# Attention weights loaded by transposing DMA: halves of 2048 columns (rows of 4 KB) in place of quarters of 1024

## The chip, the cores and the metric

The kernel runs on one core of one Trainium2 chip. The metric is the device time of one execution in microseconds (us). The kernel before takes 1625.06 us, the median of 3 runs (1622.38 to 1628.38). In what follows, SBUF is the core's working memory, PSUM the eight accumulator banks that TensorE writes, and the granted clock the share of the full TensorE clock that the profile records. A load lands when its last byte has arrived.

## The reference, cut to what matters

Two layers of a segment-recurrent attention (part A) alternate with two gated feed-forward blocks (part B). Part A walks over 64 segments of 32 tokens and hands 8 memory rows from one segment to the next, which makes a long serial chain.

```python
def _A_ref(x, mem0, Wq, Wk, Wv, Wo, seg_len):      # Wq, Wk, Wv: (448, 16, 256); Wo: (16, 256, 448); bf16
    mem = mem0
    for s in range(n_seg):                         # 64 segments
        h = jnp.concatenate([mem, x[:, s * 32:(s + 1) * 32]], axis=1)
        q, k, v = (jnp.einsum('btd,dhe->bhte', h, W) for W in (Wq, Wk, Wv))
        p = softmax(masked(q @ k) / 16)
        o = jnp.einsum('bhte,hed->btd', p @ v, Wo)
        mem = o[:, :8]                             # to the next segment
        ...
x = x + A(layernorm(x)); x = x + B(layernorm(x)); x = x + A(layernorm(x)); x = x + B(layernorm(x))
```

## The kernel before

The kernel never forms q, k and v. In a set-up it folds the weights, head by head, into M = Wq Wk^T and N = Wv Wo, and then works with M and N only. Both products contract over a head's 256 columns, so Wq, Wk and Wv are needed with those columns on the partitions. A transposing DMA does that on the way in. Each of the three matrices arrives in four pieces of 1024 columns (four heads), Wo in four plain pieces, all issued by SyncE on one queue.

```python
        def load_t(w, q):
            S.q.add("dma", ("sp",), {"sp": 3600.0}, lambda E: E.dma_start_transpose(out=st[w, q], in_=src[w][:, q * 1024:(q + 1) * 1024]),
                    (), [(w, q)], name=f"{w}{q}", lat=2500.0)

        def load_o(q, wr=()):
            S.q.add("dma", ("sp",), {"sp": 3000.0}, lambda E: E.dma_start(st["Wo", q], S.Wo_d[:, q * 8:q * 8 + 8, :]),
                    (), [("Wo", q)] + list(wr), name=f"Wo{q}", lat=2500.0)
        # ... cut ...
        for q in range(4):
            load_t("Wq", q)
            load_t("Wk", q)
        # ... cut: small loads, masks, and the products of M, for pairs of heads i = 0..7, each of which
        #     reads ("Wq", i // 2) and ("Wk", i // 2) ...
        for q in range(4):
            load_t("Wv", q)
            load_o(q, [("Wk", q)] if q > 1 else [])     # Wo 2 and 3 take the place of Wk 2 and 3
        def n_main(q):
            for h in range(4 * q, 4 * q + 4):
                for kt in range(3):
                    T = S.tile("R", 1)                  # one of the eight PSUM banks
                    S.mm(lambda T=T, h=h, kt=kt: full("Wv", "Wo", h, kt, T), 2 * S.pitch(D), [("Wv", q), ("Wo", q)], T.res() + [("stage",)])
                    S.cp(...)                           # ScalarE or VectorE moves the bank into N
```

Nothing runs in the order in which it is written. Every operation is put into a list with what it reads and writes and with a guess of its cost in ns (`3600.0` above is the guess for a quarter). A list scheduler on the host then plays these costs through and fixes the order of each engine's instructions:

```python
    def program(self):
        self.q = _Order(self.sc)
        self.setup()
        for t in range(NSTEP):
            self.step(t)
        self.q.run()        # the order of every engine, from the cost guesses
        self.q.emit()       # instructions and semaphore waits, in that order
```

So a changed cost guess may reorder every engine, even where no instruction changed. Three small transposes follow the same queue in every step, from SBUF to SBUF: `xAT` and `xBT` (normalised tokens) and `PTs` (softmax rows).

## Time and profile before

| | before |
|---|---|
| median of 3 runs | 1625.06 us |
| span of the profiled run | 1622.9 us |
| TensorE busy | 95% |
| SyncE issues without a gap | 0.74 to 59.6 us |
| first product of M | 11.19 us |
| first product of N | 42.94 us |
| first product that uses N (N x UTm, where UTm holds rows of h weighted by the softmax) | 78.77 us |

The last three rows are the landmarks; everything up to the last of them is called the set-up.

From the page of before: the span, the busy time of TensorE ("PE": us, share, instructions), and then rows of 40 equal slices of 40.6 us each, busy tenths for TensorE and GB/s of the DMA engines.

```profile
span 1622.9 us, 67486 instructions
...
PE 1548.5 (95%) x30194; PEld 1116.4 (69%) x30194; DVE 1071.2 (66%) x2987; ACT 717.3 (44%) x2164; POOL 90.6 (6%) x156
...
PE   6889999999999999999999999999999999999996
...
GB/s 220 209 79 22 14 16 16 19 18 14 15 19 15 17 16 19 18 14 18 15 15 17 16 19 18 15 14 18 15 17 18 16 19 14 18 14 14 17 21 16
```

TensorE is busy for 90% or more from the third slice to the last but one; only the first two slices leave room, and there alone the DMA row shows more than 200 GB/s. The loads of Wq, Wk, Wv and Wo are all in them.

From the timeline of SyncE of before. Columns: start us, how long SyncE was held by the issue, queue, line, operation, tiles, count.

```profile
0.74 3.96 SPq L534 DMA_TRANSPOSE Nw<-in_A_Wq_dram  x1
4.76 4.29 SPq L534 DMA_TRANSPOSE Nw<-in_A_Wk_dram  x1
...
32.66 4.58 SPq L534 DMA_TRANSPOSE big<-in_A_Wv_dram  x1
37.28 0.59 SPq L538 DMA_DIRECT2D big<-in_A_Wo_dram  x1
37.92 6.20 SPq L534 DMA_TRANSPOSE big<-in_A_Wv_dram  x1
44.17 0.58 SPq L538 DMA_DIRECT2D Nw<-in_A_Wo_dram  x1
...
59.08 0.53 SPq L538 DMA_DIRECT2D big<-in_A_Wo_dram  x1
59.65 2.20 SPq L764 DMA_TRANSPOSE xAT<-xn  x1
```

SyncE is held for about 4 us by each quarter; the first, with no load ahead of it, is held as long as the others, and the profile does not show what holds it. From 32.66 us on quarters alternate with plain Wo loads (0.6 us of issue), and each quarter that has a Wo load ahead of it holds SyncE for 6 to 7 us.

From the timeline of TensorE of before. Columns: start, duration, engine, line, operation, out<-in, shape, count, and in brackets how long TensorE had been idle and what ended it.

```profile
11.19 5.89 PE L128 MATMUL b<-Nw 128*128 128x448 bf16 x18 [4.62 <-DMA Nw<-in_A_Wk_dram]
...
29.78 5.82 PE L128 MATMUL b<-big,Nw 128*128 128x448 bf16 x32
36.49 5.80 PE L128 MATMUL b<-big,Nw 128*128 128x448 bf16 x32 [0.90 <-issue]
42.94 4.70 PE L128 MATMUL b<-big 128*128 128x448 bf16 x24 [0.64 <-issue]
50.66 6.78 PE L128 MATMUL b<-Nw,big 128*128 128x448 bf16 x28 [3.02 <-issue]
...
66.35 0.24 PE L128 MATMUL b<-hT,Mw 128*128 128x40 bf16 x3 [0.26 <-DVE hT L703]
...
78.77 1.51 PE L128 MATMUL b<-Nw,UTm 128*32 128x448 bf16 x28 [0.64 <-ACT UTm L702]
```

The products of M begin when the first Wk quarter has landed (11.19). Those of the fourth quarter wait 0.90 us (36.49), those of N 0.64 us for Wo 0 and 3.02 us for Wo 1. "issue" there means that the profile shows no releaser; the moment fits the landing of the load named. At 66.35 the first step begins.

### The profile page before, as it was taken

How to read it: one execution, taken by the hardware profiler on the slowest of the kernel's cores; microseconds unless marked ns; L12 is line 12 of the kernel's file. 1: busy time of each engine (PE TensorE's matmuls, PEld its weight loads, DVE VectorE, ACT ScalarE, POOL GpSimd, SP SyncE). 2: the span in 40 equal slices, each digit the busy share in tenths (PEclk: the TensorE clock that was granted, in tenths of full speed). 3: DMA queues.
4: the chain of work that ended last, by engine and by line, in shares of the span. 5: the costliest groups of instructions: out<-in, count | busy, mean ns of one | idle time of the engine just before them, and what ended most of it. 6: DMA issues, size and time to landing. Idle time of an engine off the chain costs nothing. (4 is left out here: it accounts for less than half of the span.)

```text
span 1622.9 us, 67486 instructions
## 1 busy us (share of the span) xinstructions
PE 1548.5 (95%) x30194; PEld 1116.4 (69%) x30194; DVE 1071.2 (66%) x2987; ACT 717.3 (44%) x2164; POOL 90.6 (6%) x156
## 2 busy tenths in 40 slices
PE   6889999999999999999999999999999999999996
PEld 2456767767766777677667776776677777766675
DVE  8646767666666676666675766666667666666554
ACT  5524434444443454445443444444444444534332
POOL 3100000000000000000000000000000000000000
PEclk9989999999999999999999999999999999999998
DMA  9821000100000000000000000000000000000010
GB/s 220 209 79 22 14 16 16 19 18 14 15 19 15 17 16 19 18 14 18 15 15 17 16 19 18 15 14 18 15 17 18 16 19 14 18 14 14 17 21 16
DMA packets 130289, 45.46 MB, mean 28 GB/s; under 512 B 119113, under 2 KB 129105, under 8 KB 130001
## 3 DMA queue, kind: packets, MB, share of 16 engines
q1 hardware_dynamic: 129648, 40.92, 11.8%
q8 instruction: 238, 3.90, 1.0%
q14 instruction: 51, 0.41, 0.1%
q10 hardware_dynamic: 352, 0.24, 0.1%
HBM read 10.33 MB, written 1.84 MB: 7 GB/s over the span
## 5 line engine op out<-in xcount | busy, mean ns | idle before, releaser
L128 PE MATMUL b<-hT,Mw 128*128 128x80 bf16 (+1 forms) x11424 | 440.6, 200 | 10.4 <-DVE big L703 7.8
L128 PEld LDWEIGHTS b<-hT,Mw 128*128 128x128 bf16 x11424 | 418.6, 100 | 33.2 <-DVE big L703 13.1
L128 PE MATMUL b<-Nw,big 128*64 128x448 bf16 (+1 forms) x1936 | 309.3, 357 | 4.5 <-issue 3.0
L128 PE MATMUL b<-xBT,big 128*128 128x128 bf16 (+1 forms) x3920 | 216.1, 216 | 9.6 <-DMA xBT<-xn 9.0
L128 PEld LDWEIGHTS b<-xBT,big 128*128 128x128 bf16 x3920 | 205.9, 99 | 11.7 <-DMA xBT<-xn 10.6
L703 DVE CAST TTs<-b 128x320 bf16<-128x320 f32 (+5 forms) x423 | 192.2, 454 | 31.9 <-PE b L128 30.9
L702 ACT ACTIVATE TTs<-b 64x256 bf16<-64x256 f32 (+4 forms) x461 | 191.7, 416 | 39.7 <-PE b L128 31.5
L128 PEld LDWEIGHTS b<-Nw,big 128*64 128x64 bf16 (+1 forms) x1936 | 127.2, 104 | 115.5 <-issue 24.7
L128 PE MATMUL b<-Nw,UTm 128*32 128x448 bf16 x3752 | 191.6, 355 | 1.4 <-ACT UTm L702 1.3
L702 ACT ACTIVATE TTm<-b 128x80 bf16<-128x80 f32 (+5 forms) x400 | 91.7, 229 | 224.6 <-PE b L128 223.8
L703 DVE CAST TTm<-b 128x80 bf16<-128x80 f32 (+5 forms) x484 | 111.9, 231 | 110.4 <-PE b L128 104.8
L128 PEld LDWEIGHTS b<-Nw,UTm 128*32 128x32 bf16 x3752 | 97.6, 97 | 90.1 <-issue 18.9
L703 POOL COPY hK<-xn 32x448 bf16<-32x448 bf16 x136 | 75.6, 556 | 1423.4 <-DVE xn L739 1417.1
L128 PE MATMUL b<-hT,M 64*128 64x80 bf16 (+3 forms) x3808 | 139.9, 197 | 6.8 <-DVE TTs L703 3.7
L703 DVE CAST big<-b 128x512 bf16<-128x512 f32 (+1 forms) x163 | 107.3, 675 | 58.3 <-PE b L128 57.2
L703 DVE CAST UTm<-b 128x448 bf16<-128x448 f32 (+2 forms) x107 | 64.8, 615 | 101.2 <-PE b L128 99.9
L1086 ACT ACTIVATE gT<-b 128x256 bf16<-128x256 f32 x227 | 85.5, 379 | 104.4 <-PE b L128 79.2
L128 PEld LDWEIGHTS b<-hT,M 64*128 64x128 bf16 (+1 forms) x3808 | 105.8, 97 | 22.3 <-DVE hT L703 6.7
L1087 DVE TENSOR_TENSOR hB<-gT,b 128x256 bf16<-128x256 bf16 x227 | 90.6, 411 | 42.9 <-ACT gT L1086 37.5
L702 ACT ACTIVATE big<-b 128x512 bf16<-128x512 f32 (+1 forms) x225 | 106.4, 514 | 8.4 <-PE b L128 7.5
L946 ACT ACTIVATE hi<-b 128x448 bf16<-128x448 f32 x67 | 36.4, 543 | 145.5 <-PE b L128 143.8
L702 ACT ACTIVATE UTm<-b 128x448 bf16<-128x448 f32 (+2 forms) x144 | 76.3, 552 | 39.3 <-PE b L128 37.5
(100 smaller groups left out, 1522.4 us busy)
## 6 DMA issues: line engine op xcount, KB each, us to landing
big<-in_A_Wo_dram SPq DMA_DIRECT2D x3, 896.0 KB, 5.9
out_dram<-ys SPq DMA_DIRECT2D x32, 56.0 KB, 1.9
big<-in_B_W_down_dram SPq DMA_DIRECT2D x1, 1568.0 KB, 7.1
XA<-in_A_x_dram SPq DMA_DIRECT2D x28, 56.0 KB, 2.2
big<-in_B_W_up_dram SPq DMA_DIRECT2D x1, 1344.0 KB, 7.5
big<-in_B_W_gate_dram SPq DMA_DIRECT2D x1, 1344.0 KB, 8.9
PTs<-Ps SPq DMA_TRANSPOSE x68, 2.4
Nw<-in_A_Wo_dram SPq DMA_DIRECT2D x1, 896.0 KB, 6.4
```

Of the source, the lines that this page charges most:

```text
L128: ins = E.matmul(out, lhsT=lhsT, rhs=rhs, **kw)
L702: return E.activation(out(), src(), ACT.Copy)
L703: return E.tensor_copy(out(), src())
L946: S.act(lambda E: E.activation(S.hi[:, :], C.b()[:, 0:D], ACT.Copy), D, C.res(), [("hi",)])
L1086: S.act(lambda E, k=k, R=R, n=n: E.activation(S.gT[:, k % 2, 0:n], R[0].b()[:, 0:n], ACT.Relu), n, R[0].res(), [("gT", k % 2)])
L1087: S.dve(lambda E, k=k, R=R, n=n, fcs=fcs: E.tensor_tensor(S.hB[:, fcs[0]:fcs[-1] + 1, 0:w], S.gT[:, k % 2, 0:n].rearrange("p (a b) -> p a ...
```

## The change

The intent: rows of 4 KB in place of 2 KB, and half as many transposes. A half covers eight heads. The cost guess of a half is 5300, less than two quarters at 3600.

```diff
-        def load_t(w, q):
-            S.q.add("dma", ("sp",), {"sp": 3600.0}, lambda E: E.dma_start_transpose(out=st[w, q], in_=src[w][:, q * 1024:(q + 1) * 1024]),
-                    (), [(w, q)], name=f"{w}{q}", lat=2500.0)
+        def load_t(w, i):
+
+            both = {"Wq": NW[:, 4 * i * W8:(4 * i + 2) * W8], "Wk": NW[:, 2 * W8:4 * W8] if i == 0 else BG[:, 0:2 * W8],
+                    "Wv": BG[:, (2 * i + 2) * W8:(2 * i + 4) * W8]}[w].rearrange("p (k d) -> p k d", k=16)
+            S.q.add("dma", ("sp",), {"sp": 5300.0}, lambda E: E.dma_start_transpose(out=both, in_=src[w][:, i * 2048:(i + 1) * 2048]),
+                    (), [(w, 2 * i), (w, 2 * i + 1)], name=f"{w}{i}", lat=2500.0)
...
-        for q in range(4):
-            load_t("Wq", q)
-            load_t("Wk", q)
+        for i in range(2):
+            load_t("Wq", i)
+            load_t("Wk", i)
...
         for q in range(4):
-            load_t("Wv", q)
+            if q % 2 == 0:
+                load_t("Wv", q // 2)
             load_o(q, [("Wk", q)] if q > 1 else [])
```

## The prediction

> **What bounds the kernel now.** TensorE is busy 95% of the 1622.9 us span (busy shares). The change touches only the set-up, about the first 78 us, in which Wq, Wk, Wv arrive transposed in twelve quarters and Wo in four plain loads, all issued by SyncE, which the timeline shows issuing without a gap from 0.74 to 59.6 us.
>
> A Wq or Wk quarter (0.92 MB) takes 4.0 us of the queue (eight from 0.74 to 32.6 us) and lands 6 to 7 us after its issue. Fine slices of the DMA row show about 290 GB/s for 3.2 us, then a dip of 0.7 to 0.9 us. Small transposes fit: 32 tiles of 4 KB take 1.2 us, 224 tiles 4.0, so roughly 0.75 us fixed and 14.4 ns a tile.
>
> TensorE's waits on these loads (its timeline): until 11.19 us for the first products; 0.9 us at 36.5 (Wk quarter 3); 0.6 at 42.9 (Wo 0); 3.0 at 50.6 (Wo 1, behind a Wv quarter); 0.7 at 58.2; 0.5 at 65.5 (Wo 3). After 35 us that is 5.8 us. Another 2.9 us, before 20 us, is not a load's: the PSUM banks are full while VectorE builds masks until 18.8.
>
> **What the change does.** Six transposes of 1.84 MB replace twelve. Six fixed parts fall away, about 4.5 us. If the rate per tile stays, a half takes 0.75 + 448 x 14.4 ns = 7.2 us instead of 8.05. The rows double to 4 KB: the Trainium skill, "DMA: Bandwidth & Descriptors", section "Latency and other measured facts", gives 261 GB/s for a transpose that misses the 4 KB concatenation of its reads, 350 to 400 for a contiguous one. At 350 a half would take 5.9 us. The trace of before (229 GB/s, dips included) agrees with the low figure; no run yet shows the high one. My estimate: 6.3 us a half.
>
> Against it: the first product needs both first halves and starts at about 15.5 us, not 11.2.
>
> **On the critical path.** The later start should be nearly free: PSUM is evacuated only from 18.8 us, when the banks will just be full. Then the M stage runs at the pace of TensorE and the evacuation (2.9 us per pair of heads). The second Wk half lands at about 28 us, before it is needed (29.8). Wv and Wo then come ahead of TensorE, and the 5.8 us of waits mostly vanish. No more can be gained there, since TensorE is then the limit. At 7.2 us a half, Wk's second lands at about 32 and the gain falls to 3. What follows (Wd, Wg, first PTs) moves forward with the last N product.
>
> So 5 to 6 us: **1619 us, 80% range 1611 to 1626**. Faster by over 2%: 0.01; within 2%: 0.98; slower by over 2%: 0.01.
>
> **What would show it.** SyncE's timeline: a Wq or Wk half takes 6 to 7 us (right) or over 7.5 (no gain). DMA row: longer plateaus, at 290 GB/s (fixed cost only) or about 350 (rows). First product at 15 to 16 us; M stage ending near 42; no TensorE wait over 1 us from 36 to 66; the last N product 6 us earlier than 77.4; from 120 us on the same work, shifted.
>
> **What would make it wrong.** The instruction order is computed from cost guesses; new costs may reorder the whole program, a few us either way. Masks may still be built late, with M's evacuation pushed back. The granted clock dips to 0.5 in stretches from 84 to 102 us, and other stalls may move those dips. The times of before spread over 6 us.

## The result, and the profile after

| | before | after |
|---|---|---|
| median, same rounds, 6 runs each | 1625.31 us | 1627.15 us |
| range | 1622.29 to 1628.38 | 1622.5 to 1631.49 |
| span of the profiled run | 1622.9 us | 1625.2 us |
| first product of M | 11.19 us | 18.55 us |
| first product of N | 42.94 us | 47.63 us |
| first product that uses N | 78.77 us | 78.61 us |
| first output row issued | 266.76 us | 269.18 us |

The ratio is 1.0014 with a 95% interval of 0.9992 to 1.0036: the same. A ratio is the mean time of one kernel's fast runs over that of the other's of the same rounds, so it is not quite the ratio of the medians. A later repeat of both kernels gave 1.0025 (1.0006 to 1.0043). By these two ratios the change costs 2 to 4 us (only the second interval excludes no difference), where 5 to 6 us less had been forecast.

From the page of after, the same lines:

```profile
span 1625.2 us, 67481 instructions
...
PE 1546.5 (95%) x30194; PEld 1117.4 (69%) x30194; DVE 1070.6 (66%) x2988; ACT 719.7 (44%) x2163; POOL 91.0 (6%) x156
...
PE   4989999999999999999999999999999999999996
...
GB/s 234 197 77 21 13 17 16 19 16 16 15 19 14 18 16 19 18 14 18 15 16 17 16 19 18 14 15 19 15 17 16 19 19 14 17 14 14 17 21 16
```

The first slice has less TensorE work (4 tenths in place of 6), the second more (9 in place of 8). These shares do not say where the time went; the timelines do. The DMA row moved 234 GB/s in the first slice against 220.

From the timeline of SyncE of after:

```profile
0.74 7.82 SPq L537 DMA_TRANSPOSE Nw<-in_A_Wq_dram  x1
8.61 7.53 SPq L537 DMA_TRANSPOSE Nw<-in_A_Wk_dram  x1
...
31.75 6.96 SPq L537 DMA_TRANSPOSE big<-in_A_Wv_dram  x1
...
40.01 11.29 SPq L537 DMA_TRANSPOSE big<-in_A_Wv_dram  x1
...
52.59 10.22 SPq L768 DMA_TRANSPOSE xAT<-xn  x2
```

A half of Wq or Wk holds SyncE for 7.5 to 7.8 us, 7.75 from issue to issue on average (the four take 0.74 to 31.75 us). Two quarters took 8.0 (the eight take 0.74 to 32.66). So the halves are hardly faster per byte.

From the timeline of TensorE of after:

```profile
18.55 13.30 PE L128 MATMUL b<-Nw 128*128 128x448 bf16 x64 [12.03 <-DMA Nw<-in_A_Wk_dram]
34.56 13.14 PE L128 MATMUL b<-big,Nw 128*128 128x448 bf16 x64 [2.71 <-issue]
47.63 4.71 PE L128 MATMUL b<-big 128*128 128x448 bf16 x24
52.18 5.20 PE L128 MATMUL b<-Nw,big 128*128 128x448 bf16 x28
...
60.26 0.42 PE L128 MATMUL b<-hT,M 64*128 64x40 bf16 x20 [0.82 <-DVE hT L707]
...
78.61 1.70 PE L128 MATMUL b<-Nw,UTm 128*32 128x448 bf16 x32 [0.64 <-ACT UTm L706]
```

The first product comes 7.4 us later than before. The second Wk half is missing for 2.71 us at 34.56, and from there on all four remaining head pairs (64 products, 13.14 us) still have to be done, where in before only two pairs (5.80 us) stood behind the last landing. M therefore ends 5.4 us later (47.7 against 42.3); 1.6 us of this are a half-clock stretch, as the same 64 products took 11.55 us in another profile (after_again below). In exchange the waits for Wo are gone: N starts at 47.63 and runs on. At 60.26 there is something that the old profile does not have: TensorE turns to the first step before it has done N's third quarter, and waits for the copy of `xAT`. The first product with N then comes at the same time as before.

### The profile page after: what moved, and what is told of

Read it like the earlier page. It is cut to its first block, busy times and chain, and to the rows that moved or that the text cites. A ratio compares the mean times of both kernels' runs of the same rounds, so it can differ in the third digit from the quotient of the medians.

```text
span 1625.2 us, 67481 instructions
## 1 busy us (share of the span) xinstructions
PE 1546.5 (95%) x30194; PEld 1117.4 (69%) x30194; DVE 1070.6 (66%) x2988; ACT 719.7 (44%) x2163; POOL 91.0 (6%) x156
## 3 DMA queue, kind: packets, MB, share of 16 engines
q1 hardware_dynamic: 129456, 40.92, 11.6%
## 5 line engine op out<-in xcount | busy, mean ns | idle before, releaser
L706 ACT ACTIVATE TTs<-b 64x256 bf16<-64x256 f32 (+4 forms) x461 | 191.6, 416 | 38.8 <-PE b L128 30.7
```

Of the source, the lines that this page charges most:

```text
L706: return E.activation(out(), src(), ACT.Copy)
```

## The experiments

Four explanations stood at the start. **A (grain):** a half costs nearly two quarters, and coarser arrival leaves more work behind the last landing of M, while the stage of Wv and Wo wins about as much. **B (order):** the loads did bring a gain, and the order that came with the new guess of 5300 ate it. **C (rows):** rows of 4 KB stream faster, and the kernel merely hides it. **D (clock):** a wait of TensorE costs twice, because the granted clock drops after it. A fifth, **E**, came out of an experiment.

To separate loads from order, most kernels below keep the scheduler's result of before for all engines and rewrite only the list of SyncE's loads afterwards:

```diff
         self.q.run()
+        self.reshape_loads()     # merges quarters of HALVES into halves, or permutes the loads; nothing else
         self.q.emit()
```

A comparison of the instructions in the traces confirms for each of these that TensorE, VectorE, ScalarE and GpSimd have the same order as before (f_v_fill adds its 18 products), and that SyncE differs in the loads alone.

### f_all_halves: all halves, old order

```diff
+    HALVES = ("Wq", "Wk", "Wv")
```

> All twelve quarters become six halves, but every other engine keeps the instruction order of before exactly. Theory A (arrival grain: a half takes twice a quarter's time less about 0.35 us, so the rows of 4 KB buy nothing; the last Wk half has four head pairs of work behind it where the last quarter had two, which costs 5 us in the M stage; the Wv/Wo stage then wins the same back): halves of Wq/Wk occupy the queue 7.6 to 7.8 us, first weight product at 18.5 us, M stage ends at 47.5, first product of N with UTm at about 78.6 to 79 us (before 78.77), time equal to before within 0.3%. Theory B (the gain was there and was eaten by the new order that the new cost guess 5300 brought): with the old order the first UTm product comes at 73 to 76 us and the time falls by 3 to 5 us.

Measured: median 1625.62 us, ratio 0.9991 (0.9963 to 1.0018). First product 18.54, first of N 45.35, first with N **75.96 us**. Theory A alone had said 78.6 to 79, and missed; theory B's 73 to 76 holds, while the 3 to 5 us less in the time that it also named are not seen (the ratio stands for 1.5 us less, with an interval from 6 less to 3 more). With the old order the halves do bring the set-up forward.

### f_qk_halves and f_v_halves: one part of the change each

```diff
+    HALVES = ("Wq", "Wk")        # f_qk_halves
+    HALVES = ("Wv",)             # f_v_halves
```

> Only Wq and Wk come in halves, Wv stays in quarters; all other engines in the order of before. Theory A: the M stage ends at about 47.5 us as in the changed kernel (before 42.3), the Wv/Wo stage has hardly any wait left because it starts late, so the first UTm product is at 78.5 to 80 us: no gain, at most 1 us loss. Theory B: as f_all_halves, some gain.

> Only Wv comes in halves, with Wo 0 and 1, then 2 and 3, in one go behind them; Wq and Wk stay in quarters; all other engines in the order of before. Theory A: M stage ends at 42.3 us as before, N products start at about 45 us (before 42.9) as Wo 0 now waits for a half, but then run without the 3.0 us wait; last N product about 73.5, first UTm product 75.5 to 76.5 us (before 78.77): 2 to 3 us saved, 0.15% of the time. Theory B predicts the same as for f_all_halves here.

Measured: f_qk_halves has its first N product at 44.15 and the first with N at 76.70 us, 2.1 us before the kernel before: better than expected (ratio 0.9985, 0.995 to 1.0019). f_v_halves has them at 45.96 and 79.03: worse than expected by 3 us (ratio 1.0005, 0.9979 to 1.0031). The reason for that miss stands in the next two views of f_v_halves: one line of TensorE's timeline, and two stretches of 4 us (columns: stretch, length, busy us and count of each engine, granted clock, DMA share, GB/s).

```profile
45.96 7.17 PE L128 MATMUL b<-big 128*128 128x448 bf16 x24 [3.93 <-issue]
```

```profile
44.00:48.00 4.00, 2.04 (x6) 0.89 (x7) 0.34 (x1) 0.54 (x1) 0.00 (x0) 0.52 1.13 345
48.00:52.00 4.00, 4.00 (x14) 1.70 (x13) 1.87 (x4) 1.63 (x3) 0.00 (x0) 0.62 1.24 279
```

TensorE waited 3.93 us for Wo 0, and then the 24 products of N's first quarter took 7.17 us. In before they took 4.70. The granted clock was 0.52 and 0.62 in these stretches.

### f_v_fill: TensorE kept busy through that wait

The same kernel with 18 idle products into the PSUM tile that the first real N product overwrites:

```diff
                 if o.kind == "pe":
+                    if o.cat == "first N":   # 18 products of 448 columns, reading Wq 3 and Wk 3, before the wait for Wo 0
+                        self.sc.pe(self.filler(o), [("Wq", 3), ("Wk", 3)], res(o.wr))
```

> f_v_halves plus 18 idle products (448 columns, 3.4 us in all) that TensorE does before it waits for the first Wo, into the PSUM tile that the first real N product overwrites. In f_v_halves the wait of 3.93 us there was followed by a stretch of 6.8 us at granted clock 0.5, in which 24 N products took 7.17 us in place of 4.7. Theory D (the stall costs twice, once as the wait and once more as the lower clock that follows it): with the fillers the clock stays at 1, the 24 products take 4.7 us and the first UTm product comes at 76 to 77 us (79.03 without). If the lower clock has another cause, 79 us as before.

```profile
45.72 4.70 PE L128 MATMUL b<-big 128*128 128x448 bf16 x24 [0.69 <-DMA big<-in_A_Wo_dram]
```

```profile
44.00:48.00 4.00, 3.31 (x19) 1.52 (x18) 1.19 (x2) 1.27 (x3) 0.00 (x0) 1.00 1.17 307
48.00:52.00 4.00, 4.00 (x23) 2.08 (x22) 3.20 (x7) 2.93 (x6) 0.00 (x0) 1.00 1.27 290
```

The same 24 products took 4.70 us at clock 1.00, and the first product with N came at 77.09 us in place of 79.03. Theory D holds for this wait: of the cost of the stall, 2.5 us were the clock. The Trainium skill, "TensorE: Matmul & The Clock Gate", Part 1, says that the clock falls to half after an idle window of about 3.4 us. The traces agree with the half (0.5 in the clock record) and with such a window (the low stretches here are 3.4 us or multiples of it), but not with idle, as after_again below shows.

But the whole run took **1654.37 us**, ratio 1.0193 (1.0167 to 1.022): slower by 1.9%, with an interval that reaches over 2%. Nothing in the steady part differs from f_v_halves in order. This is taken up below (theory E).

### f_grouped: the order of the loads alone

```diff
+    GROUP = ["Wv0", "Wv1", "Wo0", "Wo1", "Wv2", "Wv3", "Wo2", "Wo3"]     # quarters, all
```

> All loads stay quarters of 1024 columns; only SyncE's issue order changes to Wv0 Wv1 Wo0 Wo1 Wv2 Wv3 Wo2 Wo3, the order that the halves bring by themselves. Theory A1 (the Wv/Wo stage gains because there are fewer turns from a transpose to a plain load and back, each a dip of the DMA row): as f_v_halves less 0.7 us, first UTm product at 76 to 77 us, no row of 4 KB needed. Rival A2 (it gains because a half is itself cheaper there): first UTm product at 78 to 79 us, as before.

Measured: first of N 46.31, with N 79.66 us, ratio 0.999 (0.9966 to 1.0013). Neither number fits. N's start was again delayed, here by a wait of 4.30 us for Wo 0, and again a half-clock stretch followed (24 products in 7.45 us). So grouping is not free: the first Wo comes behind two Wv quarters. What it saves in turns between transposes and plain loads is measured without such disturbance in the next run.

### loads_alone: the disputed cost by itself

A kernel that does nothing but load, group after group, each group landed before the next begins. Its output is wrong, which doesn't matter for the time.

```python
for n in (1024, 2048, 4096, 512, 1024, 2048):  group(Wq and Wk in transposes of n columns)      # 7.3 MB each
for _ in range(2):  group(T P T P T P T P); group(T T P P T T P P); group(H P P H P P)          # 7.3 MB each
group(P P P P)
```

> Nothing but weight loads, in groups that land before the next starts; the output is zeros, wrong on purpose. Groups of 7.3 MB of Wq and Wk in transposes of 1024, 2048, 4096, 512, 1024, 2048 columns; then 7.3 MB of Wv and Wo as T P T P T P T P, T T P P T T P P, H P P H P P (T a quarter, H a half, P a plain Wo load), each twice; then P P P P. Theory A (the rate inside a transpose is fixed at about 290 GB/s whatever the row; wider pieces save only the dip between two transposes): groups of 1024 take 8 x 4.0 = 32 us, of 2048 4 x 7.5 = 30, of 4096 2 x 14.3 = 29, of 512 16 x 2.4 = 38; plateaus 290 GB/s in all. Theory C (rows of 4 KB stream faster, and the whole kernel only hides it): groups of 2048 and 4096 take 22 to 25 us with plateaus near 350. Turns between transposes and plain loads cost dips: T P alternating about 27 us plus the final landing, T T P P about 25, H P P about 24.

Measured, from the first issue of a group to that of the next (one look, state unknown):

| group | us | per half, or two quarters |
|---|---|---|
| 16 transposes of 512 | 37.68 | |
| 8 of 1024 (quarters) | 32.81 and 32.41 | 8.2 and 8.1 |
| 4 of 2048 (halves) | 30.96 and 30.17 | 7.7 and 7.5 |
| 2 of 4096 | 28.52 | |
| T P T P T P T P | 30.21 and 30.86 | |
| T T P P T T P P | 28.75 and 28.83 | |
| H P P H P P | 27.40 and 27.52 | |

One line each of the DMA row over a window of this run: quarters (0 to 20 us, slices of 0.5 us), then 4096 columns (65 to 92 us, slices of 0.68 us), then plain loads and the output (358 to 388 us, slices of 0.75 us).

```profile
GB/s 0 0 0 0 87 230 291 288 274 290 290 155 85 220 289 280 268 292 283 120 192 289 276 209 264 291 237 112 125 290 289 289 289 292 208 109 231 290 263 230
```

```profile
GB/s 0 104 286 273 291 290 291 291 289 291 290 291 291 290 289 291 290 291 290 289 144 78 286 291 291 290 289 290 291 291 289 290 290 291 291 289 291 290 290 291
```

```profile
GB/s 289 290 120 276 326 336 344 382 382 240 47 6 0 81 238 381 381 378 381 378 379 382 381 379 382 381 354 38 0 200 257 213 247 214 245 225 236 228 231 153
```

With quarters the row reaches 290 and falls every 4 us. With 4096 columns it stays at 290. It never goes over 292 in either, and the groups of 512 and of 2048 columns reach the same 290. Plain loads reach 380. So the rate inside a transpose does not depend on the row from 1 to 8 KB, and a wider piece saves only the dip between two transposes. Theory C is refuted. The groups with Wo came out 3 to 4 us longer than expected, in the expected order: fewer turns are worth 1.4 to 2.1 us per 7.3 MB, halves about another 1.4. From one issue to the next within a group, a half took 6.6 to 7.6 us here, 7.1 on average, where the halves of Wq and Wk in the whole kernels took 7.0 to 8.0.

### after_again: the changed kernel once more

> The changed kernel unaltered, for a second profile and a better mean. If the half-clock stretch after the 2.7 us wait for the second Wk half (35.8 us) comes by chance, its first UTm product will now be at 76 to 77 us; if that wait always brings it, at 78.6 us again. In the time: ratio 0.998 to 1.002.

Measured: median 1628.52, ratio 1.0025 (1.0006 to 1.0043). From TensorE's timeline of this profile:

```profile
33.16 11.55 PE L128 MATMUL b<-big,Nw 128*128 128x448 bf16 x64 [1.19 <-issue]
44.65 4.71 PE L128 MATMUL b<-big 128*128 128x448 bf16 x24
...
60.64 0.52 PE L128 MATMUL b<-hT,M 64*128 64x40 bf16 x20 [4.18 <-DVE hT L707]
...
81.16 2.83 PE L128 MATMUL b<-Nw,UTm 128*32 128x448 bf16 x56 [0.64 <-ACT UTm L706]
```

This time the wait for Wk was 1.19 us, no half clock followed it, and M's second part took 11.55 us (13.14 in the first profile). N started at 44.65, 3 us earlier. And still the first product with N came at **81.16**, later than in the first profile and than either expectation. All that was won was lost in one wait of 4.18 us at 60.64, on the copy of `xAT`. The clock was at half for 6.8 us from 60.0 us. In both profiles the first step begins at 60.3 to 60.6 us: that is when `xAT` has landed, behind Wv and Wo on the queue, and TensorE's order does not let it do N's third quarter meanwhile.

Whether half clock follows a wait is less a matter of chance than it looks. In the 17 profiles of whole kernels, all 112 half-clock stretches begin on a grid with steps of 3.413 us that is fixed within a profile (in before at 19.75, 50.47, 84.61 and 91.43 us, which are 9, 10 and 2 steps apart). Between the first product of M and 66 us, half clock followed all 19 steps in which TensorE was busy for 46% of the time or less, and of the steps at 48% or more only those that were at half clock themselves. The wait of 2.71 us in after lay mostly in one step (36% busy); the 2.90 us in after_cost were shared by two (56 and 59%), and no half clock followed. The shares use the modelled ends of products, and the bound holds for the large products of the set-up alone.

### f_order_only: the new order with the old loads

The changed kernel's order for TensorE, VectorE, ScalarE and GpSimd; loads as quarters, issued in the order of before.

```diff
         self.q.run()             # with load_t as in the changed kernel
+        self.split_loads()       # each half back into two quarters, SyncE's order of before
         self.q.emit()
```

> The converse: TensorE, VectorE, ScalarE and GpSimd in the order of the changed kernel, but the loads as quarters and issued in the order of before. Theory B2: TensorE waits for the first transposed x, which lands at about 66 us here, before N's third quarter, so the first UTm product comes at 83 to 86 us and the time is 4 to 7 us above before. If the order is harmless: 78 to 79 us.

```profile
64.15 0.51 PE L128 MATMUL b<-hT,M 64*128 64x40 bf16 x20 [7.38 <-DVE hT L741]
...
83.72 2.83 PE L128 MATMUL b<-Nw,UTm 128*32 128x448 bf16 x56 [0.64 <-ACT UTm L740]
```

Measured: first of N 41.85, then 7.38 us of waiting for `xAT`; first with N at **83.72 us**; median 1630.37, ratio **1.0040** (1.0021 to 1.006). By the ratio the new order alone costs about 6 us (3 to 10). Theory B's mechanism is shown, with its place.

### after_cost: the change with an honest guess

```diff
-            S.q.add("dma", ("sp",), {"sp": 5300.0}, ...
+            S.q.add("dma", ("sp",), {"sp": 7700.0}, ...
```

> The changed kernel with one number altered: the cost guess of a half is 7700 ns, which is what a half takes, instead of 5300, so the instruction order is computed from arrival times that the chip keeps. Theory B2 (half of what the change lost is the order: the guess of 5300 makes TensorE stand before N's third quarter waiting for the first transposed x, which lands only at 60 us): no TensorE wait on that transpose over 1 us, first UTm product at 75.5 to 77 us (78.6 and 81.2 in the two profiles of the changed kernel, 78.77 before), time 2 to 4 us below the changed kernel. If the order does not matter: 78.5 to 81 us and the same time.

Measured: no wait on `xAT`, first with N at 76.89 us (78.61 and 81.16 with the guess of 5300), median 1626.44, ratio 1.0006 (0.9992 to 1.0019). The wait is removed by this one number. By the ratios the time is 1 to 3 us better than that of the changed kernel (1.0014 and 1.0025), which the overlapping intervals do not make certain, and it is not better than before.

### f_mixed: first halves, then quarters

The one candidate that the findings suggested: coarse where TensorE cannot start anyway, fine where M's tail hangs on it, and halves for Wv.

```diff
+    HALVES = (("Wq", 0), ("Wk", 0), ("Wv", 0), ("Wv", 1))
```

> Wq and Wk: the first half as one piece, the second in quarters; Wv in halves; all other engines in the order of before. Theory A (grain: the last arrival decides, with the work behind it): first product at 17.8 to 18.5 us, no wait before the third quarter's heads, M stage ends at 43.5 to 44 us (f_all_halves 45.3), N products without a wait over 0.5 us, first UTm product at 74.3 to 75 us (before 78.77, f_all_halves 75.96). In the time 3 to 4 us less than before, 0.2%, just at what five rounds resolve.

Measured: M ran without a wait and ended at 43.55, as expected; but Wo 0 was missing for 1.86 us and N started at 45.41. First with N 77.08 (expected 74.3 to 75). Median 1627.97, ratio 1.0021 (1.0002 to 1.004). It does not beat before, and its interval overlaps those of the changed kernel.

### f_all_again and f_qk_again: does the earlier set-up reach the end?

> f_all_halves unaltered, for a second profile and a better mean: halves for all weights with the order of before. If its earlier first UTm product (75.96 us, 77.5 to 78.8 with quarters in the order of before) is real and reaches the end: again 75.5 to 77 us, and a ratio of 0.997 to 0.9995. If it is given back on the way to 267 us (a late transposed xB, stretches at half clock): the early product again, but a ratio of 0.9995 to 1.001.

> f_qk_halves unaltered (halves for Wq and Wk alone, order of before), the same question: first UTm product 76 to 77.5 us, ratio 0.9975 to 1.0 if the gain reaches the end. Both hypotheses leave the sum of set-up terms as it is; only what follows differs.

Measured: f_all_again has the first product with N at 76.61 and a ratio of 1.0009 (0.9993 to 1.0025); f_qk_again 76.03 and 1.0005 (0.9987 to 1.0022). So the earlier product is real, and no gain is seen at the end. But 1.8 us are 0.11% of the time, and these intervals reach 0.16% or more to each side: they cannot say for certain that it is lost. By landmarks, each as us from the landmark before:

| profile | first with N | to first output row | to 29th output row | to the end |
|---|---|---|---|---|
| before | 78.77 | 187.99 | 1297.13 | 59.0 |
| after | 78.61 | 190.57 | 1297.42 | 58.6 |
| after_again | 81.16 | 188.98 | 1297.42 | 58.3 |
| f_all_halves | 75.96 | 190.35 | 1297.08 | 58.3 |
| f_all_again | 76.61 | 191.21 | 1297.45 | 60.7 |
| f_qk_halves | 76.70 | 188.00 | 1297.99 | 58.6 |
| f_qk_again | 76.03 | 188.95 | 1298.34 | 59.2 |
| after_cost | 76.89 | 191.47 | 1300.46 | 58.0 |
| f_order_only | 83.72 | 186.10 | 1297.68 | 59.6 |

With all halves, the stretch to the first output row is 2.4 to 3.2 us longer than in before. This may be scatter: in the four shift runs below, which keep quarters and the order of before, it is 186.6 to 191.3 us. One place of a loss is seen in the traces. From the views of tile `xBT` between 115 and 135 us (time from issue to landing, the first of its kind), of before, and then of f_all_again with TensorE's line:

```profile
DMA to landing us min/median/max: 2.4/2.4/2.4
```

```profile
DMA to landing us min/median/max: 3.9/3.9/3.9
```

```profile
128.20 3.34 PE L128 MATMUL b<-xBT,big 128*128 128x64 bf16 x64 [1.32 <-DMA xBT<-xn]
```

In before this small transpose landed in 2.4 us and TensorE did not wait. In f_all_again, in f_all_halves and in after it took 3.9 us, TensorE waited 1.26 to 1.32 us, and a half-clock stretch of 3.4 us followed (the granted clock from 120 to 132 us was 0.86 in all three, 1.00 in before). In these three a fetch of 16 KB of instructions began 1.8 to 1.9 us after the issue of `xBT`; in before none was in flight. The next section shows that such a fetch delays small transposes. The part from 84 to 104 us, where the clock is half for 7 to 14 us in every profile, is not resolved: it varies from profile to profile of one kernel by more than what is sought.

### shift_36, shift_256, shift_128, shift_200: why a filler cost 28 us

Between first and 29th output row f_v_fill took 1325 us where all kernels in the table above took 1297 to 1300. The four kernels here are the kernel before with 18, 128, 64 or 100 tiny products at about 6 us, when TensorE is idle anyway. A product is two instructions (a weight load and a matmul), so TensorE's stream is shifted by 36, 256, 128 and 200 instructions.

```diff
         for o in self.order:
+            if o.kind == "pe" and first:
+                first = False
+                self.sc.pe(self.filler(o), [("ident",)], res(o.wr))     # n products of 32 columns
```

> The kernel before plus 18 tiny products (36 instructions) on TensorE at about 6 us, while it waits for its first weights anyway. The run with the fillers lost 28 us in the steady part with the same order, where the 16 KB instruction fetches moved into the flight of small transposes. Theory E (a shift of TensorE's stream by 36 instructions does it, whatever the instructions are): set-up as before (first UTm product 78 to 80 us), but 1645 to 1660 us in all. If the fillers' place or their large matrices did it: 1620 to 1630 us.

> As shift_36 with 128 tiny products, 256 instructions, which at 64 bytes each is one whole fetch of 16 KB. Theory E: all fetches fall where they fell before, 1620 to 1631 us. If every shift costs: over 1640 us.

> The kernel before plus 64 tiny products (128 instructions, half a fetch). Theory E (where the 16 KB fetches fall against the small transposes decides): a time that differs from before by several us in either direction, with the spread of xAT, xBT and PTs landings to match; not 1656 by rule. If only the number of extra instructions mattered, over 1656.

> The same with 100 tiny products (200 instructions). Theory E: another time, between 1615 and 1660, not monotone in the count: 0, 36, 128, 200, 256 instructions.

Measured (one look each, state unknown; set-up as before in all, first product with N at 77.5 to 78.7 us):

| shift, instructions | time us | first to 29th output row, us | small transposes with a fetch in flight: mean us to landing (count) | without: mean, longest | TensorE's waits for small transposes, us |
|---|---|---|---|---|---|
| 0 (before) | 1625.06 | 1297.1 | 2.89 (29) | 2.43, 3.07 | 1.7 |
| 36 | 1655.94 | 1327.0 | 3.27 (43) | 2.42, 2.77 | 26.6 |
| 128 | 1649.60 | 1316.8 | 3.54 (53) | 2.43, 2.83 | 20.8 |
| 200 | 1628.32 | 1299.9 | 2.92 (56) | 2.42, 2.81 | 4.0 |
| 256 | 1622.65 | 1296.6 | 2.71 (33) | 2.42, 2.82 | 1.3 |

The last three columns are taken from the traces between 270 and 1560 us: a fetch is a packet of 16 KB on the instruction queue, in flight if it overlaps the time from the transpose's issue to its landing; the last column adds TensorE's waits for `xBT`, for `PTs` and for VectorE's copy of `xAT`. Against before, these waits rise by 24.9, 19.1, 2.3 and -0.4 us, and the stretch from the first to the 29th output row by 29.9, 19.7, 2.8 and -0.5. Without a fetch in flight, no small transpose of any profile took over 3.1 us. With one, they took up to 4.5. A shift of 256 brings the old time back, so it is not the number of extra instructions. The Trainium skill, "Runtime: NRT & Kernel Launch", section "Instruction fetch mechanics", says that the stream is refilled in blocks of 16 KiB, 256 instructions; the trace agrees on the size, and the run with 256 agrees with the period. From the waits of TensorE (us in total, times, longest) and the view of tile `xAT`, both from 270 to 1560 us, first of before and then of shift_36:

```profile
PE b L128 <- DVE hT L703: 0.5, 1, 0.5
```

```profile
  DMA xAT<-xn: 7.3, 14
...
DMA to landing us min/median/max: 2.4/2.4/3.1
```

```profile
PE b L128 <- DVE hT L708: 18.0, 14, 1.6
```

```profile
  DMA xAT<-xn: 28.5, 27
...
DMA to landing us min/median/max: 2.4/2.6/4.3
```

In shift_36, VectorE stood 28.5 us in all for the landing of `xAT` (7.3 in before), and TensorE behind it 18.0 us, in 14 waits of up to 1.6 us that the kernel before has once. Theory E is shown: what matters is where the fetches of TensorE's stream fall against the small transposes for which TensorE waits. The mere number of slowed transposes does not decide: there are more of them with a shift of 200 than of 36. Each shift is a single run; f_v_fill, also shifted by 36 and measured four times (1652 to 1659 us), repeats the first.

## Why the prediction was wrong, point by point

**Failed: "My estimate: 6.3 us a half."** This is the mis-sized term on which the rest was built. A half took 7.75 us on average in the changed kernel, and 7.1 in loads_alone. The gain in rate for 4 KB rows, taken from the skill's 350 to 400 GB/s for a contiguous transpose, is not there: 290 GB/s inside the transpose at every width from 512 to 4096 columns. The prediction read 229 GB/s as agreeing with the page's low figure of 261, although its own slices of 290 lay above that. The fall-back of 7.2 us, from a straight line through two sizes (1.2 us for 32 tiles, 4.0 us for 224), fits loads_alone; so does 2 x 0.92 MB / 290 GB/s + 0.8 us of dip = 7.1 us. The changed kernel's halves add about half a microsecond that these traces do not explain.

**Failed, in consequence: "The second Wk half lands at about 28 us, before it is needed".** It landed at 34.5 and 33.1 us in the two profiles of the changed kernel. Its products started at 33.2 to 34.6 us, after waits of 1.2 to 2.7 us, and four head pairs, 11.6 us at full clock, stood behind it. In before two pairs, 5.8 us, stood behind the last quarter. N started at 44.7 and 47.6 us rather than at about 42.

**Right in mechanism: "the 5.8 us of waits mostly vanish".** With the old order, the stretch from N's first product to the first with N shrank from 35.8 us to 30.6 and 30.7 (f_all_halves, f_all_again). The five profiles with quarters in the old order (before and the four shifts) have the first product with N at 78.1 us on average, the two with halves at 76.3. So M loses 3.1 us (N's start is 45.6 against 42.5 on the same averages), the stage of Wv and Wo gains 4.9, and 1.8 us are the net of the halves themselves. Six had been forecast. Of the 4.9, about 1.6 are no wait: in before a half-clock stretch after the wait for Wo 1 made 28 products take 6.78 us (5.20 in after).

**Failed by omission: the order.** "The instruction order is computed from cost guesses; new costs may reorder the whole program" was named as a risk and left out of the sum. In the set-up it turned the gain into a loss: the guess of 5300, 2.4 us under what a half takes, makes the scheduler believe in an early `xAT` and lets TensorE stand before N's third quarter. Alone it costs about 6 us (f_order_only, ratio 1.0040); in the changed kernel there were 0.8 and 4.2 us of wait in the two profiles. The first product with N came, on average, at 78.1 us with quarters and 76.3 with halves in the old order, and at 83.7 (one profile) and 79.9 in the new. With 7700 in place of 5300 the wait is gone. In the traces the order differs between 24 and 75 us alone, so the fear of a reordered steady part was unfounded.

**Half right: "The later start should be nearly free".** The first product came at 18.5 us, 3 us after the forecast, and evacuation would have begun at 18.8. By the end of the first 64 products, 31.85 against 29.85 us, it had cost 2.0 us. The first products took 0.37 us each in both kernels, and 0.19 later, although the clock record reads 1.00 there; in before this slow start was over by the time TensorE waited for full banks.

**Not borne out: "What follows (Wd, Wg, first PTs) moves forward with the last N product."** In the changed kernel that product did not come earlier. With all halves in the old order the first product with N did, by 1.8 us, but the first output row came at 266.3 and 267.8 us, and at 264.2 to 270.0 in the five profiles with quarters. A late `xBT` with a fetch in flight, and the half-clock stretch after it, are seen with halves, but in shift_36 with its quarters too; how much they cost, against the unsteady clock between 84 and 104 us, stays open.

**Right:** within 2%, no change in the steady part (1297.1 to 1297.4 us for 28 output rows in both kernels), and the granted clock as a source of error of this size.

The ledger of the changed kernel against before, from two profiles of after and one of before: +1.1 us at the first product with N, +1.8 to the first output row, +0.3 to the 29th, -0.6 to the end, together +2.6 us; the ratios say +2 to +4. Its parts lie within what single profiles scatter; the sum and the terms named above are what is shown.

## What to carry to other kernels

Making a load coarser saves only the gap between two loads, if the rate inside one is already flat, and it puts twice the work behind the last landing: ask which consumer waits for the last piece and how much is left to do then. Where an order is computed from guesses, a changed load needs a measured guess, or the order takes back more than the load gives. Before a gain of a few microseconds is believed, or a loss of many is put down to the edit, the same edit should be tried with the instruction stream shifted: 36 idle instructions cost this kernel 2%, 256 nothing.

## What the Trainium skill lacked or had wrong

- "DMA: Bandwidth & Descriptors", section "Latency and other measured facts", gives 350 to 400 GB/s for a contiguous transpose, and "Advanced Engine Details and Errata", section "X-Bar Transpose (TRN2)", calls transposes as fast as plain DMAs. Here transposes from HBM reach 290 GB/s and no more for rows of 1, 2, 4 and 8 KB, plain loads reach 380. With the gaps, 7.3 MB came at 195 GB/s (512 columns), 225 (1024), 240 (2048) and 257 (4096), each 7.34 MB over the group's time.
- No page has the cost of a turn between transposes and plain loads on one queue: alternating quarters took 30.2 to 30.9 us for 7.3 MB, in pairs 28.8.
- "Runtime: NRT & Kernel Launch", section "Instruction fetch mechanics", says that the fetch is hidden behind the pace at which instructions are dispatched. It has nothing on what a fetch does to other transfers: here a small transpose with a 16 KB fetch in flight took 2.7 to 3.5 us on average against 2.4, and the place of the fetches moved the time between 1622.65 and 1655.94 us.
- "TensorE: Matmul & The Clock Gate", Part 1, ties the half clock to an idle window of about 3.4 us. The windows are seen here (a grid of 3.413 us), but they need not be idle: in the set-up a step with TensorE busy for 46% was enough (f_grouped at 14.4 us), and before the stretches at 125 to 129 us, where the products are smaller, steps of 61 to 74% were (f_all_again, after, f_all_halves).
